# Other due times for visits, block sums and first halves, and other normalisers for five groups, in a planned attention and feed-forward kernel

## The chip, the cores and the metric

The kernel runs on one core of a Trainium2 chip. The time is device microseconds of that core for one execution. Before the change it was 583.85 us, the median of three runs (583.55 to 584.67).

## The reference

Attention over 4 batches of 8 heads, 768 tokens and 64 numbers a head, then a feed-forward part over the 3072 tokens with 512 features and 2048 hidden ones. All inputs are float32.

```python
k_sum = k.reshape(B, H, nb, block, D).max(axis=3)      # block = 32
v_sum = v.reshape(B, H, nb, block, D).mean(axis=3)
scores_l = scale * np.matmul(q, k.transpose(0, 1, 3, 2))
mask_l = np.abs(pos[:, None] - pos[None, :]) < window   # window = 16
scores_s = scale * np.einsum('bhsd,bhnd->bhsn', q, k_sum) + np.log(block)
scores_all = np.concatenate([np.where(mask_l, scores_l, -1e9), scores_s], axis=-1)
a = np.exp(scores_all - np.max(scores_all, axis=-1, keepdims=True))
a = a / (np.sum(a, axis=-1, keepdims=True) + 1e-09)
x = np.matmul(a, np.concatenate([v, v_sum], axis=2))    # then tokens x 512
h = x @ w_in
r = np.maximum(h, 0.0)
out = (r * r) @ w_out
```

## The kernel before, in words

The 3072 tokens are cut into 48 groups of 64. Eight groups make a unit of 512 tokens. A *visit* on TensorE does the scores of coming groups (L756) and the values of earlier ones (L997) in one go. Around a visit the other engines work on a group: the vector engine masks the scores and takes the row maximum (L830), ScalarE takes exponentials (L887), the vector engine the reciprocal of the sum (L899, L900). Then a group is normalised, either by one vector instruction (L906) or by four on ScalarE (L913); the string `NORMAL_BY` has a letter for each of the 48 groups, D or A. The result is turned for the next matmul, by TensorE and a copy (L926, L933) or by the vector engine and DMAs (L955, L970, L975). The outcome of a visit is cut into a high part `xh` (ScalarE, L1062) and a low part `xl` (vector engine, L1065).

The feed-forward matmuls are of high and low parts in three terms, to keep float32's precision. The first two units, called plain, go through 16 tiles f of the hidden features. For each there are 12 hidden matmuls (L1195) into one of two PSUM banks `h`; ScalarE applies relu (`rl`, L1204), squares in place (L1205) and makes the high part `gh` (L1206); the vector engine makes the low part `gl` from both (L1209); 12 outer matmuls (L1219) follow. There is one buffer `rl`: relu of the next tile can start only when `gl` of this one is done. The visits' results and the groups turned on TensorE use the two PSUM banks of `h` too. The remaining four units go by a scheme with fewer matmuls that needs sums of blocks of the weights (L1731 and L1514). These sums are made while the plain units run: GpSimd adds whole blocks (L1300, L1315), ScalarE and the vector engine split them (L1318, L1321); half sums (L1364, L1379) are GpSimd's for five of the eight pairs and the vector engine's for pairs 4, 6 and 7 (`HALF_SUMS_BY`), split at L1382 and L1385; SP stores them (L1324, L1390) in device memory. In the same stretch the weights come in (L1125) and are split (L1128, L1131, L1137, L1142, L1145), and the keys' block maxima are taken (L566).

In what order an engine does all this is not written by hand. Every piece of work is given to a planner (class `Plan`) with an engine, an estimated duration, the work it comes after, the buffers it takes and a *due time*. The planner plays the program through: whenever an engine is free, it starts the ready piece with the earliest due time. The result is one fixed order for each engine, which the chip keeps: a piece that isn't ready holds up all behind it on its engine. The due times come from tables of numbers in us: `VISITS` (visits, and with them all work on their groups), `COMBS` (block sums of pairs, L1288), `SUMS` (half sums, L1916), `HALF_AT` (the first halves of the first unit, L1105 and L1176), `FV_AT` (loads of the values of the later batches, L597), `Q_LEAD` (query loads, L1747) and `X_LEAD` (splits of a visit's outcome, L1085). A changed number moves whatever takes part in the same competition, also work that the table doesn't name.

```python
t2 = add(f"RL{name}", "ACT", act, lambda: nc.scalar.activation(cut(r), cut(h), AF.Relu), due + 3, [t1], take=[r], use=[h])
...
if NORMAL_BY[g] == "A":
    t_n = add(f"N{g}", "ACT", 1.2, normal_by_act, due - 10, [t_r], use=[pr, nm])
else:
    t_n = add(f"N{g}", "DVE", 0.56, normal, due - 10, [t_r], use=[pr, nm])
```

Of the kernel before, what the change touches and what calls it, by code (L numbers as in the profile page):

```python
# [44 lines left out]
HIGH_DVE = 0  # L45
ONE_EXP = 1
RUN1, RUN2, RUN4 = (1 + 218 / n for n in (1024, 2048, 4096))
NORMAL_BY = "DDDDDDDDDDDDAADDDDDAADDADDAAAADDADDDDAADAAAAAAAA"
HALF_SUMS_BY = "PPPPDPDD"
TURN_BY = "PPPPDPDDPDDDDDDDDDDDDDDD"  # L50
LAG = 2
PLAIN = 2
RINGED = 4
PRODUCTS = 7
FV_AT = 60.61, 233.96
FV1_LEAD = 17.0
HALVED = 2
TURN_LATE = 0.4
COMBS = 113.9, 126.8, 141.39, 159.1, 177.9, 210.24, 223.15, 214.82
Q_LEAD = 10.72  # L60
XS_LEAD = 10
R_LEAD = 9
TR_LEAD = 16.82
VISITS = 50.65, 58.31, 70.31, 76.15, 99.76, 110.62, 136.36, 142.89, 161.01, 177.12, 203.05, 215.03, 227.83, 233.26, 248.89, 277.47, 296.02, 310.51, 324.02, 346.69, 366.69, 366.74, 394.74
X_LEAD = 5.36
SPLIT_AT = -7.62
KEPT = 105.02, 3.08
GH_LEAD = 12
# [258 lines left out]
def attention_then_relu2_ffn(  # L327
# [96 lines left out]
    T0, SLOW, STEP = 28.0, 6.4, 6.7  # L424
    MIXED_STEP = 1.54, 1.41
    X_BY = 19.41, 14.78
    SUMS = 121.7, 129.74, 148.43, 166.33, 195.88, 201.13, 197.53, 197.25, 153.98, 169.96, 168.64, 165.29, 173.06, 198.45, 180.64, 190.85
    PRODUCT_STEP = 1.51, 1.34
    A0, A1, B0, B1 = 12.0, 2.0, 21.0, 2.2
    HALF_AT = 26.97, 32.0  # L430
    MX = 0.95
    steps = [SLOW, STEP]
    unit_at, mixed_at, products_at, at = [], [], [], T0
# [11 lines left out]
    def wanted(g):  # L445
# [5 lines left out]
        if g < APART:  # L451
            return VISITS[i] if g % 2 else (VISITS[i] + (VISITS[i - 1] if i else VISITS[0] - 20)) / 2
        return VISITS[i - 1] + 17 - 5 * (g % 2 == 0)

# [3 lines left out]
    def visited(g):  # L458

        return VISITS[(g - UG) // 2 + (g >= APART - 2)] if g >= UG else wanted(g)  # L460

# [134 lines left out]
    def batch_v(b):  # L596
        key = FV_AT[b - 2] if b > 1 else visited(b * NW - 1) - FV1_LEAD if b else -60  # L597
        out_ps = h_buf(f"vps{b}")
# [207 lines left out]
    def softmax(g, by_pe=False):  # L806
# [107 lines left out]

        if NORMAL_BY[g] == "A":
            t_n = add(f"N{g}", "ACT", 1.2, normal_by_act, due - 10, [t_r], use=[pr, nm])
# [86 lines left out]
    def visit(both, then=(), block_sums=None):  # L1003

        n, g = len(both), (both or (-1,))[-1]
        due = visited(g) if both else VISITS[(then[0] - UG) // 2 - 1]
        x_ps = h_buf(f"x{g}") if n == 2 else x_buf(f"x{g}") if n else None
# [278 lines left out]
    def combine(p):  # L1286

        due = COMBS[p]  # L1288
        ws = [woven[1, 2 * p + k] for k in range(2)]
# [374 lines left out]
    def mixed(s):  # L1664
# [26 lines left out]
        def product(p, j, o, begins, deps, also=(), taken=False):  # L1691
# [54 lines left out]
            n += 1  # L1746
            return t, due + 1.5 - Q_LEAD  # L1747

# [165 lines left out]
    for p in FOLDED:  # L1914
        for k in range(2):
            combine_in(p, k, SUMS[2 * p + k])  # L1916
    for s in range(NS):
# [69 lines left out]
```

## Time and profile before

| | us |
|---|---|
| median of three runs | 583.85 |
| the profiled execution | 583.48 |
| its span, first to last instruction | 581.0 |
| TensorE busy | 563.0 (97%) |
| vector engine busy | 452.2 (78%) |
| ScalarE busy | 373.7 (64%) |
| GpSimd busy | 134.5 (23%) |
| mean granted clock of TensorE | 0.996 |

The span is the profile's; 2.48 us of the execution's own time lie around it. A row of a timeline gives the start in us, the time until the last instruction of the row ended, the engine, the line, the operation, output and inputs with their shapes, and how many instructions the row holds. What stands in brackets is the idle time of the engine ahead of the row and what ended it. PE is TensorE, DVE the vector engine, ACT ScalarE, POOL GpSimd, SPq the queue of SyncE, which issues the DMAs. The plain units run from about 30 to 260 us, the rest behind.

### The profile page before, as it was taken

The page shows a single profiled execution, that of the slowest core. Times are in us where ns is not written, and L with a number is a line of the kernel's source. Part 1 is how long each engine was busy: PE and PEld are TensorE (multiplying, and loading weights), DVE is VectorE, ACT ScalarE, POOL GpSimd, SP SyncE. Part 2 cuts the span into 40 slices and gives each one's busy share as a digit, 9 for nine tenths or more (in the row PEclk, how much of TensorE's full clock was granted, in tenths as well). Part 3 has the DMA queues.
Part 4 walks back from the last instruction along what each step waited for, and adds up shares of the span by engine and source line. Part 5 has one row for each costly group of instructions (what it writes and reads, how often), then busy time and mean ns, then how long its engine had stood idle before and what let it go on. Part 6 is the DMA issues. An engine that isn't in the chain of part 4 may idle for free.

```text
span 581.0 us, 12047 instructions
## 1 busy us (share of the span) xinstructions
PE 563.0 (97%) x4052; PEld 460.2 (79%) x4052; DVE 452.2 (78%) x1015; ACT 373.7 (64%) x968; POOL 134.5 (23%) x193
## 2 busy tenths in 40 slices
PE   7879999999999899999999999999999999999997
PEld 6668787888887688887888888888888888888885
DVE  4899999685799997879976978869932656868864
ACT  1899899786757787768765768464634642454442
POOL 4300010167669469500043430000000000000000
PEclk9999999999999999999999999999999999999999
DMA  8899996989997999999988888866875566667672
GB/s 298 295 382 340 332 337 243 323 327 341 304 381 236 327 358 338 364 333 335 312 271 246 268 257 257 268 181 192 256 240 175 178 195 192 196 195 226 196 227 98
DMA packets 88082, 157.15 MB, mean 270 GB/s; under 512 B 9066, under 2 KB 30926, under 8 KB 88022
## 3 DMA queue, kind: packets, MB, share of 16 engines
q1 hardware_dynamic: 88022, 156.39, 82.2%
q8 instruction: 32, 0.52, 0.4%
q14 instruction: 28, 0.23, 0.1%
HBM read 111.30 MB, written 44.66 MB: 268 GB/s over the span
## 4 chain that ended last, share of the span: by engine, by line
PE 76%; DVE 9%; DMA 8%; SPq 3%; issue 2%; ACT 1%; DVEq 0%; ACTq 0%
PE o L1514 23%; PE o L1731 14%; PE h L1195 9%; PE o L1219 9%; PE sz L1731 8%; PE att L1514 4%; PE x L997 3%; DMA raw<-wW 3%; PE att L756 2%; PE sa L1731 2%; PE att L1731 2%; DMA v<-vS 1%; DMA fv_lent<-vS 1%; DMA out<-os 1%; DVE ci L1379 1%
## 5 line engine op out<-in xcount | busy, mean ns | idle before, releaser
L1496 ACT CAST gh<-g 128x512 fp32r<-128x512 f32 x112 | 69.3, 621 | 63.2 <-DVE gl L1501 30.5
L1514 PE MATMUL o<-gh,w 128*128 128x512 f32 x384 | 103.0, 390 | 0.0
L1501 DVE TENSOR_TENSOR gl<-g,gh 128x512 fp32r<-128x512 f32 x112 | 76.8, 693 | 22.9 <-ACT gh L1496 22.4
L1514 PEld LDWEIGHTS o<-gh,w 128*128 128x128 f32 x384 | 71.8, 188 | 15.0
L1195 PE MATMUL h<-xh,w 128*128 128x512 f32 x240 | 76.2, 399 | 3.9 <-ACT rl L1204 3.9
L1768 ACT ACTIVATE g<-g 128x512 f32<-128x512 f32 x60 | 37.6, 630 | 49.5 <-DVE g L1764 49.3
L887 ACT ACTIVATE p<-p,small 128x118 f32<-128x118 f32 x160 | 61.1, 387 | 1.6 <-DVE small L830 1.6
L1219 PE MATMUL o<-w,gh 128*128 128x512 f32 x240 | 61.9, 394 | 0.0
L1514 PE MATMUL o<-gl,w 128*128 128x512 f32 x192 | 59.2, 389 | 0.0
L1195 PEld LDWEIGHTS h<-xh,w 128*128 128x128 f32 x240 | 45.1, 191 | 14.2 <-ACT rl L1204 4.7
L1219 PEld LDWEIGHTS o<-w,gh 128*128 128x128 f32 x240 | 44.4, 188 | 9.7 <-issue 0.4
L1195 PE MATMUL h<-xl,w 128*128 128x512 f32 x120 | 47.2, 394 | 0.0
L1514 PEld LDWEIGHTS o<-gl,w 128*128 128x128 f32 x192 | 36.0, 188 | 7.6
L1731 PE MATMUL o<-w,w 128*128 128x512 f32 x160 | 40.6, 390 | 0.0
L769 POOL COPY kb<-kb 128x96 f32<-128x96 f32 x25 | 10.9, 435 | 107.1 <-PE att L756 36.4
L1774 POOL TENSOR_TENSOR g<-g 128x512 f32<-128x512 f32 x16 | 22.6, 1418 | 53.7 <-ACT g L1768 53.1
L1731 PEld LDWEIGHTS o<-w,w 128*128 128x128 f32 x160 | 30.0, 188 | 6.3
L1491 DVE TENSOR_TENSOR g<-g 128x512 f32<-128x512 f32 x48 | 33.9, 716 | 1.2 <-POOL g L1774 0.7
L830 DVE CUSTOM_DVE_ANT_0 p<-att,mask 128x118 f32<-128x118 f32 x152 | 32.5, 272 | 2.6 <-PE att L756 2.6
L1731 PE MATMUL sz<-xh,w 128*128 128x512 f32 x128 | 34.5, 391 | 0.0
L1219 PE MATMUL o<-w,gl 128*128 128x512 f32 x120 | 33.6, 389 | 0.0
L1764 DVE CUSTOM_DVE_ANT_0 g<-sz,g 128x512 f32<-128x512 f32 x32 | 21.9, 685 | 13.2 <-ACT g L1751 6.4
(201 smaller groups left out, 1186.7 us busy)
## 6 DMA issues: line engine op xcount, KB each, us to landing
raw<-wW SPq DMA_DIRECT2D x32, 512.0 KB
w<-scr_t SPq DMA_DIRECT2D x64, 256.0 KB
w<-scr_s SPq DMA_DIRECT2D x64, 256.0 KB
w<-scr_a SPq DMA_DIRECT2D x48, 256.0 KB
w<-scr_i SPq DMA_DIRECT2D x44, 256.0 KB
turn<-a SPq DMA_DIRECT2D x18, 512.0 KB
scr_t<-ci SPq DMA_DIRECT2D x16, 512.0 KB
v<-vS SPq DMA_DIRECT2D x34, 192.0 KB
```

The source lines that it names most:

```text
L830: nc.vector.tensor_tensor_reduce(out=pr.tile[:, j, :KEYS], in0=score_at(g, 0, j), in1=mask_of(g)[0], scale=-SCALE, scalar=-NEG, op0=ALU.ad ...
L887: nc.scalar.activation(x, score_tile(g, p % parts)[:, p] if by_pe else x, AF.Exp, bias=nm.tile[:, p : p + 1], scale=SCALE if by_pe else -1 ...
L1195: nc.tensor.matmul(cut(h), lhsT=lhs.tile[:, k // 2, k % 2 * P : (k % 2 + 1) * P], rhs=rhs[:, k, c0 : c0 + n], start=(i == 0), stop=(i == 3 ...
L1219: nc.tensor.matmul(o_of(o, t).rearrange("p (h c) -> p h c", h=2), lhsT=terms[i][0].tile[:, (t - t0) * P : (t - t0 + 1) * P], rhs=terms[i][ ...
L1491: lambda x=x, ins=ins, op=op: nc.vector.tensor_tensor(out=x.tile, in0=ins[0].tile, in1=ins[1].tile, op=op),
L1496: f"GH{s}_{n}", "ACT", 0.54, lambda x=x, gh=gh: nc.scalar.copy(out=gh.tile, in_=x.tile), due - GH_LEAD, ready,
L1501: lambda x=x, gh=gh, gl=gl: nc.vector.tensor_tensor(out=gl.tile, in0=x.tile, in1=gh.tile.bitcast(F32), op=ALU.subtract),
L1514: nc.tensor.matmul(o.tile[:, d], lhsT=chunk.tile[:, w * HALF + d * P : w * HALF + (d + 1) * P], rhs=y.tile, start=begins and w == 0 and y ...
L1731: nc.tensor.matmul(o.tile, lhsT=lhs(w, k), rhs=y[k], start=begins and i == 0, stop=i == 5, skip_group_check=not begins,)
L1764: lambda: nc.vector._custom_dve(TENSOR_ADD_SAT, out=to.tile, in0=o.tile, in1=x.tile, s0=HUGE, s1=0.0), key, deps,
L1768: f"G{name}_{s}", "ACT", 0.63, lambda: nc.scalar.activation(to.tile, to.tile, AF.Square), key + 0.7, [t], use=[to]
L1774: f"{name}_{s}", engine, cost, lambda: tensor.tensor_tensor(out=to.tile, in0=a.tile, in1=b.tile, op=ALU.subtract), key, deps,
```

## The change

Only numbers of the tables and five letters change; the instructions on TensorE are as many as before. Groups 12, 27, 28, 46 and 47 are normalised by the vector engine instead of ScalarE. `FV_AT` goes from 60.61, 233.96 to 53.99, 235.63; `Q_LEAD` from 10.72 to 9.51; `X_LEAD` from 5.36 to 6.51; the tenth of `SUMS` from 169.96 to 176.4; `HALF_AT` from 26.97 to 23.74 in its first number. Five of the eight `COMBS` become 3.87 to 8.79 earlier. Of `VISITS`, five get later by 0.94 and two earlier by 5.33 and 0.2.

```diff
-NORMAL_BY = "DDDDDDDDDDDDAADDDDDAADDADDAAAADDADDDDAADAAAAAAAA"
+NORMAL_BY = "DDDDDDDDDDDDDADDDDDAADDADDADDADDADDDDAADAAAAAADD"
...
-FV_AT = 60.61, 233.96
+FV_AT = 53.99, 235.63
...
-COMBS = 113.9, 126.8, 141.39, 159.1, 177.9, 210.24, 223.15, 214.82
-Q_LEAD = 10.72
+COMBS = 113.9, 126.8, 132.6, 155.23, 174.03, 206.37, 219.28, 214.82
+Q_LEAD = 9.51
```

What this does to the order is seen in three places. The names in the rows are the program's tiles: `gl_4` is the low part of hidden tile f = 4, the last number only counts the tiles of the whole program and differs between the two kernels; `kb` holds the keys and their block maxima, `raw`, `t` and `w` are weights on the way, `ci` the half sums, `cr` and `cs` the block sums.

The first place is the vector engine in the first unit. Before, at `gl_4`:

```order
L906 TENSOR_TENSOR p_82<-p_82,small_87 128x4x118
L1137 SCALAR_TENSOR_TENSOR t_929<-t_929,raw_811 128x1024
L899 TENSOR_SCALAR small_88<-small_88 128x4
L900 RECIPROCAL small_88<-small_88 128x4
L566 TENSOR_REDUCE kb<-kb 128x24
L906 TENSOR_TENSOR p_83<-p_83,small_88 128x4x118
L566 TENSOR_REDUCE kb<-kb 128x24 x2
L1209 TENSOR_TENSOR gl_4_1078<-rl_4_1045,gh_4_1060 128x512
L566 TENSOR_REDUCE kb<-kb 128x24
```

Now:

```order
L1137 SCALAR_TENSOR_TENSOR t_939<-t_939,raw_812 128x1024
L906 TENSOR_TENSOR p_83<-p_83,small_88 128x4x118
L1145 TENSOR_TENSOR w_1019<-t_915,w_1019 128x4x256
L1131 TENSOR_SCALAR raw_876<-raw_876 128x1024
L566 TENSOR_REDUCE kb<-kb 128x24
L1209 TENSOR_TENSOR gl_4_1083<-rl_4_1033,gh_4_1067 128x512
L566 TENSOR_REDUCE kb<-kb 128x24 x2
L1145 TENSOR_TENSOR w_1058<-t_939,w_1058 128x4x256
L566 TENSOR_REDUCE kb<-kb 128x24
```

The second and third key reductions have moved behind `gl_4`, and a weight piece ahead of the first.

The second place is the vector engine in the second unit, at `gl_3`, ahead of the first masking (L830) of the groups of one visit. Before:

```order
L1209 TENSOR_TENSOR gl_2_2245<-rl_2_2207,gh_2_2238 128x512
L566 TENSOR_REDUCE kb<-kb 128x24 x3
L1209 TENSOR_TENSOR gl_3_2280<-rl_3_2248,gh_3_2277 128x512
L1364 TENSOR_TENSOR ci_0_2286<-w_1133 128x2x128
L1364 TENSOR_TENSOR ci_0_2286<-w_1179 128x2x128
L1379 TENSOR_TENSOR ci_0_2286<-ci_0_2286 128x128 x4
L1385 TENSOR_TENSOR ci_0_2286<-ci_0_2286 128x4x128
L1209 TENSOR_TENSOR gl_4_2353<-rl_4_2288,gh_4_2351 128x512
L1321 TENSOR_TENSOR cr_2274<-cr_2274 128x2x256
L830 ISA p_82,small_72<-att_68,mask_76 128x118
```

Now:

```order
L1209 TENSOR_TENSOR gl_2_2251<-rl_2_2212,gh_2_2239 128x512
L1364 TENSOR_TENSOR ci_0_2255<-w_1149 128x2x128
L1364 TENSOR_TENSOR ci_0_2255<-w_1216 128x2x128
L1379 TENSOR_TENSOR ci_0_2255<-ci_0_2255 128x128 x4
L566 TENSOR_REDUCE kb<-kb 128x24
L1209 TENSOR_TENSOR gl_3_2285<-rl_3_2257,gh_3_2280 128x512
L1385 TENSOR_TENSOR ci_0_2255<-ci_0_2255 128x4x128
L1209 TENSOR_TENSOR gl_4_2348<-rl_4_2306,gh_4_2313 128x512
L830 ISA p_82,small_72<-att_68,mask_76 128x118
```

The half sums of pair 4 stand ahead of `gl_3` instead of behind it, two of the three reductions have gone to an earlier place, and the block-sum remainder `cr` (L1321) has gone behind the masking. The buffer of these half sums is the one that held the third and fourth output piece of the first unit (stored at L1262) before, and now the one that held the first and second.

The third place is some 35 us further on in the second unit, at `gl_7` on the vector engine. Before:

```order
L1379 TENSOR_TENSOR ci_0_2566<-ci_0_2566 128x128 x4
L955 STREAM_TRANSPOSE a_2609<-p_83 128x4x128
L1364 TENSOR_TENSOR ci_0_2657<-w_1684 128x2x128
L1364 TENSOR_TENSOR ci_0_2657<-w_1665 128x2x128
L1385 TENSOR_TENSOR ci_0_2566<-ci_0_2566 128x4x128
L1379 TENSOR_TENSOR ci_0_2657<-ci_0_2657 128x128 x4
L1209 TENSOR_TENSOR gl_7_2672<-rl_7_2614,gh_7_2659 128x512
L1321 TENSOR_TENSOR cr_2499<-cr_2499 128x2x256
```

Now:

```order
L1385 TENSOR_TENSOR ci_0_2419<-ci_0_2419 128x4x128
L1379 TENSOR_TENSOR ci_1_2569<-ci_1_2569 128x128 x4
L1321 TENSOR_TENSOR cr_2497<-cr_2497 128x2x256
L1321 TENSOR_TENSOR cs_2498<-cs_2498 128x2x256
L1385 TENSOR_TENSOR ci_1_2569<-ci_1_2569 128x4x128
L1364 TENSOR_TENSOR ci_0_2633<-w_1591 128x2x128
L1209 TENSOR_TENSOR gl_7_2699<-rl_7_2637,gh_7_2657 128x512
L1379 TENSOR_TENSOR ci_0_2633<-ci_0_2633 128x128 x4
```

The four sums of pair 7 (L1379, the last `ci`) have moved behind `gl_7`, the two remainders `cr` and `cs` of pair 4 ahead of it. On ScalarE, which does relu of tile 8 after `gl_7`, stood before:

```order
L913 ACTIVATE p_83<-p_83,small_72 128x118 x4
L1205 ACTIVATE rl_7_2614<-rl_7_2614 128x512
L1318 CAST cr_2499<-cr_2499 128x2x256
L1382 CAST ci_0_2566<-ci_0_2566 128x4x128
L1206 CAST gh_7_2659<-rl_7_2614 128x512
L1318 CAST cs_2500<-cs_2500 128x2x256
L1382 CAST ci_0_2657<-ci_0_2657 128x4x128
L1204 ACTIVATE rl_8_2709<-h_8_2616 128x512
```

and now:

```order
L1382 CAST ci_0_2419<-ci_0_2419 128x4x128
L1318 CAST cs_2498<-cs_2498 128x2x256
L1204 ACTIVATE rl_7_2637<-h_7_2543 128x512
L1205 ACTIVATE rl_7_2637<-rl_7_2637 128x512
L1206 CAST gh_7_2657<-rl_7_2637 128x512
L1382 CAST ci_1_2569<-ci_1_2569 128x4x128
L1204 ACTIVATE rl_8_2705<-h_8_2608 128x512
```

The normaliser of group 27 (L913) has gone from ScalarE, and the cast of pair 7's half sums has moved behind `rl_8`.

## Rows read from the trace of the kernel before

**Rows 1.** Part 1 of the page: busy time, share of the span, and instructions.

```profile
PE 563.0 (97%) x4052; PEld 460.2 (79%) x4052; DVE 452.2 (78%) x1015; ACT 373.7 (64%) x968; POOL 134.5 (23%) x193
```

**Rows 2.** The table of windows, of stretches chosen by hand. Columns: stretch, its length, busy time and instructions of PE, PEld, DVE, ACT and POOL, granted clock of TensorE, share of the DMA engines' time, GB/s.

```profile
45.00:75.00 30.00, 29.19 (x160) 23.69 (x159) 29.90 (x59) 27.93 (x62) 0.00 (x0) 1.00 0.95 342
...
135.00:165.00 30.00, 30.00 (x242) 24.56 (x241) 22.96 (x65) 22.91 (x68) 19.95 (x26) 1.00 0.93 317
...
195.00:210.00 15.00, 12.28 (x103) 9.84 (x102) 14.71 (x50) 13.81 (x44) 4.22 (x6) 0.89 0.90 316
...
345.00:576.00 231.00, 231.00 (x1127) 191.05 (x1120) 162.08 (x258) 112.08 (x203) 2.97 (x3) 1.00 0.69 207
```

**Rows 3.** What TensorE waited for: line, releaser, us in total, times, longest.

```profile
PE h L1195 <- ACT rl L1204: 3.9, 3, 2.7
...
PE o L1731 <- DVE g L1764: 0.3, 1, 0.3
```

**Rows 4.** The timeline of TensorE, 185 to 206 us.

```profile
185.29 0.73 PE L1195 MATMUL h<-xh,w 128*128 128x512 f32 x2 [0.37 <-ACT rl L1204]
...
190.86 0.62 PE L1195 MATMUL h<-xh,w 128*128 128x512 f32 x2
...
193.58 0.62 PE L1219 MATMUL o<-w,gh 128*128 128x512 f32 x2
...
201.23 1.22 PE L1195 MATMUL h<-xh,w 128*128 128x512 f32 x2 [2.72 <-ACT rl L1204]
...
205.62 0.63 PE L1219 MATMUL o<-w,gh 128*128 128x512 f32 x2
```

**Rows 5.** The timeline of ScalarE, 199 to 201 us.

```profile
199.92 0.62 ACT L1382 CAST ci<-ci 128x512 fp32r<-128x512 f32 x1 [1.00 <-DVE ci L1379]
200.58 0.60 ACT L1204 ACTIVATE rl<-h 128x512 f32<-128x512 f32 x1
```

**Rows 6.** The timeline of the vector engine, 173 to 202 us.

```profile
173.41 0.95 DVE L1321 TENSOR_TENSOR cr<-cr 128x512 fp32r<-128x512 f32 x1
174.28 0.27 DVE L830 CUSTOM_DVE_ANT_0 p<-att,mask 128x118 f32<-128x118 f32 x1
...
180.79 1.67 DVE L906 TENSOR_TENSOR p<-p,small 128x472 f32<-128x472 f32 x1
...
185.75 0.69 DVE L1065 TENSOR_TENSOR xl<-x,xh 128x512 fp32r<-128x512 f32 x1 [0.33 <-ACT xh L1062]
...
190.56 1.96 DVE L1379 TENSOR_TENSOR ci<-ci 128x128 f32<-128x128 f32 x4
...
197.64 0.71 DVE L1364 TENSOR_TENSOR ci<-w 128x256 f32<-128x256 f32 x2
...
198.88 1.01 DVE L1379 TENSOR_TENSOR ci<-ci 128x128 f32<-128x128 f32 x4
199.81 0.68 DVE L1209 TENSOR_TENSOR gl<-rl,gh 128x512 fp32r<-128x512 f32 x1
200.41 0.68 DVE L1321 TENSOR_TENSOR cr<-cr 128x512 fp32r<-128x512 f32 x1
```

**Rows 7.** The timelines of TensorE and of the vector engine, 30 to 42 us.

```profile
30.34 0.63 PE L926 MATMUL t<-ident,qvpa_lent 128*128 128x128 f32 x4 [1.76 <-DVE qvpa_lent L906]
...
40.89 0.64 DVE L906 TENSOR_TENSOR p<-p,small 128x472 f32<-128x472 f32 x1
41.44 0.41 DVE L1065 TENSOR_TENSOR xl<-att,xh 128x256 fp32r<-128x256 f32 x1
...
41.03 0.50 PE L1195 MATMUL h_0b<-xh,w 128*128 128x256 f32 x2 [1.65 <-ACT xh L1062]
```

**Rows 8.** Groups of instructions: line, engine, operation, tiles, count | busy us, mean ns of one | idle before.

```profile
L913 ACT ACTIVATE p<-p,small 128x118 f32<-128x118 f32 x80 | 24.8, 384 | 3.3 <-DVE small L900 3.3
...
L906 DVE TENSOR_TENSOR p<-p,small 128x472 f32<-128x472 f32 x20 | 17.4, 870 | 0.1
```

**Rows 9.** The timeline of all engines, 66 to 70 us.

```profile
66.71 1.80 DVE L566 TENSOR_REDUCE kb<-kb 128x24 f32<-128x768 f32 x2
...
68.43 0.68 DVE L1209 TENSOR_TENSOR gl<-rl,gh 128x512 fp32r<-128x512 f32 x1
...
69.14 0.60 ACT L1204 ACTIVATE rl<-h 128x512 f32<-128x512 f32 x1 [1.88 <-DVE gl L1209]
...
69.79 0.50 PE L1195 MATMUL h<-xh,w 128*128 128x512 f32 x1 [0.81 <-ACT rl L1204]
```

**Rows 10.** The timeline of the vector engine where it takes up the weight pieces of f = 12.

```profile
84.80 0.69 DVE L1131 TENSOR_SCALAR raw<-raw 128x1024 uint32<-128x1024 uint32 x1
```

**Rows 11.** The timelines of SP's queue, GpSimd and the vector engine, 159 to 195 us, at the half sums.

```profile
159.09 1.94 SPq L1262 DMA_DIRECT2D out<-os  x4
...
164.12 1.30 POOL L1300 TENSOR_TENSOR cr<-w 128x512 f32<-128x512 f32 x1 [7.24 <-PE o L1219]
...
166.50 1.78 DVE L1364 TENSOR_TENSOR ci<-w 128x256 f32<-128x256 f32 x2 [0.53 <-DMA out<-os]
168.31 2.92 DVE L1379 TENSOR_TENSOR ci<-ci 128x128 f32<-128x128 f32 x4
...
192.25 2.50 POOL L1379 TENSOR_TENSOR ci<-ci 128x128 f32<-128x128 f32 x4
```

**Rows 12.** The timeline of TensorE at the visit behind the half sums.

```profile
169.41 0.63 PE L756 MATMUL att<-kb,q 64*64 64x118 f32 x16
```

More of the change, by code (lines that the diff above doesn't have):

```diff
@@ L63 @@
 TR_LEAD = 16.82
-VISITS = 50.65, 58.31, 70.31, 76.15, 99.76, 110.62, 136.36, 142.89, 161.01, 177.12, 203.05, 215.03, 227.83, 233.26, 248.89, 277.47, 296.02, 310.51, 324.02, 346.69, 366.69, 366.74, 394.74
-X_LEAD = 5.36
+VISITS = 50.65, 58.31, 70.31, 76.15, 99.76, 111.56, 137.3, 143.83, 161.95, 178.06, 203.05, 215.03, 227.83, 233.26, 248.89, 277.47, 296.02, 305.18, 323.82, 346.69, 366.69, 366.74, 394.74
+X_LEAD = 6.51
 SPLIT_AT = -7.62
@@ L426, in attention_then_relu2_ffn @@
     X_BY = 19.41, 14.78
-    SUMS = 121.7, 129.74, 148.43, 166.33, 195.88, 201.13, 197.53, 197.25, 153.98, 169.96, 168.64, 165.29, 173.06, 198.45, 180.64, 190.85
+    SUMS = 121.7, 129.74, 148.43, 166.33, 195.88, 201.13, 197.53, 197.25, 153.98, 176.4, 168.64, 165.29, 173.06, 198.45, 180.64, 190.85
     PRODUCT_STEP = 1.51, 1.34
     A0, A1, B0, B1 = 12.0, 2.0, 21.0, 2.2
-    HALF_AT = 26.97, 32.0
+    HALF_AT = 23.74, 32.0
     MX = 0.95
```

## Prediction

> **What bounds the kernel now.** I read the busy shares first, then the windows, the waits of TensorE, and last the timelines at each wait. TensorE is busy 563.0 us of a span of 581.0 [rows 1], so the whole room of a change that leaves the matmuls alone is the 18 us in which it idles, plus what it loses at a lower clock. The windows say where [rows 2]: from 345 to 576 it is busy all the time; from 195 to 210 it works 12.28 of 15 us at a granted clock of 0.89, the only window below 1.00. The waits say for whom [rows 3]: one hidden matmul waited 2.7 us for ScalarE's `rl`. The timeline has it at 201.23 [rows 4]. The `rl` that it waited for ran at 200.58, behind ScalarE's `ci` cast at 199.92, which had itself waited 1.00 us for the vector engine's `ci` sums [rows 5]. Beside this ScalarE wait stands a harder one: `rl` has one buffer, which only the vector engine's `gl` frees, and that `gl` ran from 199.81 to 200.49 [rows 6]. So both causes end within 0.6 us of each other, and taking ScalarE's away alone would bring 0.1 us. Behind the `gl` lies a vector engine that was busy from 174.28 to 200.49, with 0.33 us of idle time in 26.21 [rows 6]. What has to come earlier is this row of work.
>
> The clock's price: the hidden visit after the wait took 205.62 - 201.23 = 4.39 us, against 193.58 - 190.86 = 2.72 for one at full clock, with the same 12 matmuls [rows 4]. That is 1.67 us, so the place costs 2.72 + 1.67 = 4.39 us. The waits of 1.76 and 1.65 us at the start were followed by no fall: the window from 45 on stands at 1.00 [rows 2, 7].
>
> **The change, part by part.** Instructions on TensorE are as many as before. Five groups have their normalising moved from ScalarE (four instructions of 384 ns, 1.5 us) to the vector engine (one of 870 ns) [rows 8]: 4.4 us more on the one, 7.7 less on the other. Both have room on average; only 27 stands where an engine is waited for.
>
> 1. Start (30 to 45). The second `xl` ends at 41.85, and the first-half matmuls wait for both [rows 7]. In the new order the normaliser between the two (0.64) goes behind, but two small instructions for a reciprocal come in, some 0.4: about -0.25 us. Bounds: 0 (the cast that feeds it is also late, behind an `rl`) and -1.65 (the whole wait).
>
> 2. The wait of 0.81 us at 69.79. ScalarE's `rl` waited 1.88 for `gl_4`, which stood behind two key reductions of 1.80 us in all [rows 9]. The new order sets `gl_4` ahead of these two. It can then end near 67.3, `rl` near 68.0, and TensorE comes free at 68.98 (69.79 - 0.81): the wait goes, -0.81, and nothing else is late there. Bounds 0 and -0.81. After this TensorE is 1.06 us early. I cost the rest to 155 at nothing: the window from 135 to 165 has it busy for all of its 30 us, with the vector engine busy for 22.96 [rows 2], and that spare time covers the moved work; the 1.5 MB of values that SP now issues ahead of two weight pieces are 4.4 us at the 342 GB/s of [rows 2]; of the two weight pieces the vector engine took up the first at 84.80, without an idle moment ahead of it [rows 10], so they had landed by then and have time to spare.
>
> 3. The half sums of the fifth pair (lines 1364 and 1379) and `gl_3`, 160 to 175. Before, `gl_3` ran ahead of them; now they and a reduction run ahead of it. They took 1.78 us at 166.50 and, from 168.31 to 171.23, 2.92 [rows 11]; the same at 197.64 and 198.88 took 0.71 and 1.01 [rows 6]. GpSimd was at work in the first case and had ended at 194.75 in the second [rows 11]. So the price ahead of `gl_3` lies between 1.72 and 4.70 us, and the reduction adds 0.90 (half of 1.80, [rows 9]). GpSimd begins its next sums at 164.12 when a matmul ends [rows 11], now near 163.0. The half sums' buffer was one that the third and fourth output store set free, and is now that of the first two. SP issued the four from 159.09, and the sums at 166.50 had waited for the last [rows 11]. The first two had landed by 164.12, since GpSimd's sum there wrote where they had read. In the new order they are issued about 1.5 us earlier (1.06 by the shift, 0.4 because one key load less stands ahead), so they land by 162.6. I take 161.5: the pair runs before GpSimd is at work, the four partly beside it, and `gl_3` ends near 166. Its `rl` follows 0.7 later, and TensorE needs it when the visit at 169.41 [rows 12], now 168.35, begins: no wait. Bounds: none, and the 5.4 us of the slower rival.
>
> A page of the Trainium skill speaks against this step: GPSIMD Engine Reference, section 8 "Key points", says that GpSimd shares its SBUF interfaces with VectorE, so that vector instructions with two SBUF inputs contend with it. The two durations of the four `ci` instructions, 2.92 beside GpSimd and 1.01 without it, agree. If all of the sums here were to run beside GpSimd, the page would have `gl_3` end near 168.3 and the visit wait 0.6 us, and the sum below would be 0.6 us less.
>
> 4. The row of work from the visit to `gl_7`. With the half sums out of the way the first masking begins when the visit's scores are there, about 0.95 us into it: 169.3 instead of 174.28. Between the masking and the end of `gl_7` the vector engine loses the four `ci` sums of 1.01, and gains a block-sum remainder that stood ahead of it (0.95 at 173.41), the normaliser of group 27 (0.87) and two more remainders (0.60 each, as from 199.81 to 200.41) [rows 6, 8]: 26.21 - 1.01 + 0.95 + 0.87 + 1.20 = 28.2 us, to 197.5. Bounds: 26 (the normaliser at 180.79 and the four sums at 190.56, 1.67 and 1.96, at the 0.64 of 40.89 and the 1.01 of 198.88, and 27's at 0.64 too) and 29 (27's at 1.67) [rows 6, 7], that is 195.3 to 198.3. Some waits for ScalarE and GpSimd will come in between, so I take 198.0, near the upper end. ScalarE's `rl_8` now stands directly behind a cast and no longer behind the last `ci` cast or the normaliser, so it ends at 198.7 and the matmuls start at 198.75.
>
> 5. The wait of 0.37 us at 185.29 [rows 4], for an `rl` whose `gl` belongs to the same row of work, goes: -0.37. TensorE comes to the place of [rows 4] at 198.51 - 1.06 - 0.37 = 197.1 (its wait before began at 201.23 - 2.72 = 198.51) and waits 1.65 us in place of 2.72. Earlier by 201.23 - 198.75 = 2.48 in all.
>
> 6. The clock. A wait of 1.65 lies next to the 1.76 and 1.65 that kept the clock [rows 7], and far from 2.72: I take it that it stays, -1.67. Bounds 0 and -1.67.
>
> 7. Behind it. The 0.3 us wait of a mixed product [rows 3] comes later in a row that is now ahead: -0.3, bounds 0 and -0.3. From 345 on there was no idle time to win, and 162.08 of 231 us of the vector engine were busy [rows 2], so the two normalisers there find room; if one of them delays a `gl`, that is up to 0.87.
>
> Sum: -2.48 - 1.67 - 0.3 = -4.45, from the profiled execution's own 583.48 us (span 581.0 and 2.48 around it) to 579.0. That execution lies 0.37 below the median of the runs shown, 583.85, so the median should come to 579.4. The likeliest case's own range is 578 to 580.5.
>
> **The rivals.**
> - *The clock falls all the same, or the wait comes out near 2.5.* The row of [rows 4] shows a fall after 2.72 and none after 1.76; what lies between is not shown. -2.48 - 0.3: 581.1 at the median.
> - *All the waits in the two plain units go.* If the vector engine's row from 169.3 needs 27 us or less, `rl_8` is there at about 197. -(0.25 + 0.81 + 0.37 + 2.72 + 1.67 + 0.3) = -6.12: 577.7. For it: [rows 11] show GpSimd's sums slowing the vector engine, and these now begin and end earlier. Against it: three pieces of work more stand ahead of `gl_7`.
> - *The half sums come late and hold everything: slower.* If the first output stores land only near 166.4, as the last did, the sums run wholly beside GpSimd: 166.50 + 1.78 + 2.92 + 0.90 and a `gl` of 0.68 to 0.95 put the end of `gl_3` near 173, its `rl` at 173.7, and the visit of 168.35 waits 5.4 us. The wait is longer than the 2.72 that brought the clock down, so 1.67 or more come on top, and the vector engine's row starts at 175, as late as before, with 2 us more in it. TensorE gets to the later place at 197.1 + 5.4 = 202.5, and the matmuls start near 203.6: +2.4, with the second fall of the clock up to +4. 586.3 to 587.9, say 587. It decides from a landing of about 163.4: from there `gl_3` is late by 2 to 3 us, and that with the clock's fall eats the 4.4. For it: the sums now wait for a transfer, with a DMA share of 0.93 from 135 to 165 [rows 2], and everything on the vector engine is in order. Against it: TensorE is earlier there, and the two stores are the first of four.
> - *The change does nothing that counts.* Rows are set anew in some hundred places, and new waits of a few tenths appear where the order was tight; the one at 201.23 stays at 2.7: 583.5 to 584.
>
> **How the numbers follow.** Forecast 0.43, clock falls 0.20, all gone 0.13, nothing 0.08, slower 0.16. A measurement of this kernel can tell about 0.2% from no change, 1.2 us: the limits are 582.7 and 585.0. The first three cases are faster, 0.76; the fourth is the same, 0.08; the last slower, 0.16. The range leaves out about the slower case and the lowest edge of the third: 577.3 to 584.2. The predicted time is that of the likeliest case, 579.4.
>
> **What would show it.** Right: no wait of TensorE near 69; `gl_3` of the second unit ending before 168 and no wait of the visit near 168; first masking of that visit near 169; the hidden visit after the next but one starting near 198.8 with a wait under 2 us, and a granted clock of 1.00 in the window around 200. Wrong: a granted clock below 0.95 around 200; a wait for `out<-os` on the vector engine past 163; a wait of TensorE for `gl` or `gh` behind 345, where there was none; or new waits of more than 1 us between 75 and 160, which I cost at nothing.

## The result, and the profile after

The change made the kernel slower: 588.27 us at the median of 16 runs (586.37 to 592.43), against 584.64 for the kernel before (583.55 to 588.96, 16 runs). The ratio is 1.0055, with a 95% interval of 1.0031 to 1.0080. Runs of one and the same kernel scatter over some 5 us here, so ratios with intervals carry the reading below, and a profiled execution is used for where time goes, not for how much. The profiled execution of the changed kernel, 592.34 us, is one of its longest; the one of before, 583.48, one of the shortest. Of one experiment, e_sums, the profiled execution was a disturbed one (594 us), and no time of it is read.

The page's first part and the windows of the changed kernel, with the columns of [rows 1, 2]:

```profile
PE 568.9 (96%) x4052; PEld 465.1 (79%) x4052; DVE 455.7 (77%) x1020; ACT 369.6 (63%) x948; POOL 136.0 (23%) x193
```

```profile
105.00:135.00 30.00, 28.19 (x230) 22.58 (x229) 20.27 (x59) 21.51 (x60) 10.73 (x14) 0.94 0.94 327
...
195.00:210.00 15.00, 11.60 (x98) 8.92 (x97) 14.41 (x50) 9.62 (x30) 2.92 (x5) 0.89 1.03 345
...
240.00:345.00 105.00, 100.85 (x799) 82.20 (x799) 82.40 (x222) 70.44 (x216) 25.91 (x23) 0.97 0.89 281
345.00:576.00 231.00, 231.00 (x1128) 190.90 (x1127) 163.22 (x264) 112.53 (x202) 5.17 (x4) 1.00 0.73 215
```

The window around 200 is as before (clock 0.89, 11.60 us busy where 12.28 were). Two new ones have idle time and a lower clock: 105 to 135, and 240 to 345. (From 0 to 45 the clock was 0.96, where it was 1.00; the last section takes this up.) Behind 345 nothing is lost, as before. TensorE's waits, of at least 1 us and new or changed:

```profile
PE o L1731 <- ACT os L1256: 4.1, 1, 4.1
...
PE h L1195 <- ACT rl L1204: 2.4, 1, 2.4
...
PE t L926 <- DVE small L899: 1.5, 1, 1.5
...
PE o L1219 <- DVE gl L1209: 1.0, 1, 1.0
```

The timeline of TensorE has them at four places; [rows 4, 7, 12] answer to these rows:

```profile
30.33 0.63 PE L926 MATMUL t<-ident,qvpa_lent 128*128 128x128 f32 x4 [1.72 <-DVE qvpa_lent L906]
...
118.78 0.63 PE L926 MATMUL t<-ident,p 128*128 128x128 f32 x4 [1.46 <-DVE small L899]
...
172.27 0.63 PE L756 MATMUL att<-kb,q 64*64 64x118 f32 x16
...
199.08 1.20 PE L1219 MATMUL o<-w,gl 128*128 128x512 f32 x4 [0.99 <-DVE gl L1209]
...
204.74 0.73 PE L1195 MATMUL h<-xh,w 128*128 128x512 f32 x2 [2.41 <-ACT rl L1204]
...
265.31 1.22 PE L1731 MATMUL o<-xh,w 128*128 128x512 f32 x2 [4.15 <-ACT os L1256]
```

I followed how far TensorE was from the kernel before at points where both had the same matmuls behind them; "early" and "late" mean this in what follows. It was 1.04 us early at 109, 2.87 late at 130, 3.50 late at 209 and 9.46 late at 281; nothing changed from there to the end. So two groups turned at 118.78 cost 3.9 us (1.46, a following 0.35, and a clock of 0.66 from 120 to 125); the place at 200 was about as dear as before; and the first mixed product at 265.31 cost 4.15 and about 2 us of clock.

Why these two waits came is seen on the vector engine, its timeline at the three places:

```profile
108.14 0.70 DVE L1131 TENSOR_SCALAR raw<-raw 128x1024 uint32<-128x1024 uint32 x1 [3.26 <-DMA turn<-a]
...
111.67 1.23 DVE L1145 TENSOR_TENSOR w<-t,w 128x1024 fp32r<-128x1024 f32 x1 [1.11 <-ACT w L1142]
...
117.46 1.17 DVE L906 TENSOR_TENSOR p<-p,small 128x472 f32<-128x472 f32 x1
...
165.76 0.76 DVE L1364 TENSOR_TENSOR ci<-w 128x256 f32<-128x256 f32 x2 [0.72 <-DMA out<-os]
166.56 3.22 DVE L1379 TENSOR_TENSOR ci<-ci 128x128 f32<-128x128 f32 x4
...
170.56 1.13 DVE L1209 TENSOR_TENSOR gl<-rl,gh 128x512 fp32r<-128x512 f32 x1
...
173.67 1.00 DVE L1209 TENSOR_TENSOR gl<-rl,gh 128x512 fp32r<-128x512 f32 x1 [0.83 <-ACT gh L1206]
174.59 0.27 DVE L830 CUSTOM_DVE_ANT_0 p<-att,mask 128x118 f32<-128x118 f32 x1
...
203.29 0.68 DVE L1209 TENSOR_TENSOR gl<-rl,gh 128x512 fp32r<-128x512 f32 x1
...
262.72 0.69 DVE L1256 COPY os<-o 128x512 f32<-128x512 f32 x1 [3.51 <-DMA scr_s<-cr]
```

At 108 the weight pieces of f = 15 now stand ahead of the masking of two groups, and their transfer landed only at 108.1. The row names `turn<-a`; ScalarE's row of the same moment names the weights themselves:

```profile
108.09 1.20 ACT L1128 ACTIVATE t<-raw 128x1024 f32<-128x1024 f32 x1 [3.95 <-DMA raw<-wW]
```

At 262.72 the first output piece of the second unit is to be copied out of PSUM, and its buffer is one that the block sums of pair 6 held. The store of these sums, which has to have read it, was issued on SP's queue at 257.87:

```profile
251.02 2.00 SPq L975 DMA_DIRECT2D a<-turn  x4
253.21 0.35 SPq L697 DMA_DIRECT2D q<-qW  x1
254.60 0.33 SPq L708 DMA_DIRECT2D v<-vS  x1
256.00 0.35 SPq L697 DMA_DIRECT2D q<-qW  x1
257.45 0.32 SPq L708 DMA_DIRECT2D v<-vS  x1
257.87 0.39 SPq L1324 DMA_DIRECT2D scr_s<-cr  x1
```

It stands behind the turned reads, two query and two value loads. In the kernel before it stood ahead of them and was issued at 247.03, and the copy into the buffer waited for no store:

```profile
247.03 0.49 SPq L1324 DMA_DIRECT2D scr_s<-cr  x1
...
255.27 0.65 DVE L1256 COPY os<-o 128x512 f32<-128x512 f32 x1
```

The sums themselves were later too: GpSimd ended them at 247.3 in the changed kernel, after it had stood still for 14.53 us until a store of half sums had landed:

```profile
212.60 1.01 POOL L1364 TENSOR_TENSOR ci<-w 128x256 f32<-128x256 f32 x1 [14.53 <-DMA scr_t<-ci]
...
246.61 0.73 POOL L1315 TENSOR_TENSOR cs<-cs,cr 128x256 f32<-128x256 f32 x1
```

In the kernel before it ended them at 241.2:

```profile
240.02 1.19 POOL L1315 TENSOR_TENSOR cs<-cs,cr 128x256 f32<-128x256 f32 x1
```

### The profile page after: what moved, and what is told of

It reads as the page before. It is cut to its first block, busy times and chain, and to the rows that moved or that the text cites. A ratio compares the mean times of both kernels' runs of the same rounds, so it can differ in the third digit from the quotient of the medians.

```text
span 590.5 us, 12024 instructions
## 1 busy us (share of the span) xinstructions
PE 568.9 (96%) x4052; PEld 465.1 (79%) x4052; DVE 455.7 (77%) x1020; ACT 369.6 (63%) x948; POOL 136.0 (23%) x193
## 4 chain that ended last, share of the span: by engine, by line
PE 72%; DMA 10%; DVE 7%; ACT 4%; SPq 4%; issue 2%; POOL 1%; ACTq 0%; DVEq 0%; POOLq 0%
PE o L1514 22%; PE o L1731 14%; PE sz L1731 7%; PE h L1195 7%; PE o L1219 7%; PE att L1514 4%; PE x L997 2%; PE sa L1731 2%; PE att L756 2%; DMA raw<-wW 2%; PE att L1731 2%; DMA qvpa_lent<-vF 2%; DMA scr_s<-cr 2%; DMA a<-turn 1%; DMA out<-os 1%
## 5 line engine op out<-in xcount | busy, mean ns | idle before, releaser
L1219 PE MATMUL o<-w,gh 128*128 128x512 f32 x240 | 63.1, 400 | 0.0
L769 POOL COPY kb<-kb 128x96 f32<-128x96 f32 x25 | 12.7, 508 | 110.2 <-PE att L756 36.0
L1731 PE MATMUL o<-xh,w 128*128 128x512 f32 x112 | 31.8, 408 | 4.1 <-ACT os L1256 4.1
L830 DVE CUSTOM_DVE_ANT_0 p<-att,mask 128x118 f32<-128x118 f32 x152 | 32.5, 273 | 1.0 <-PE att L756 1.0
```

The lines of the kernel that those rows point to most:

```text
L769: nc.gpsimd.tensor_copy(out=kb[:, :, nxt : nxt + NB], in_=kb[:, :, k0 : k0 + NB])
L830: nc.vector.tensor_tensor_reduce(out=pr.tile[:, j, :KEYS], in0=score_at(g, 0, j), in1=mask_of(g)[0], scale=-SCALE, scalar=-NEG, op0=ALU.ad ...
L1219: nc.tensor.matmul(o_of(o, t).rearrange("p (h c) -> p h c", h=2), lhsT=terms[i][0].tile[:, (t - t0) * P : (t - t0 + 1) * P], rhs=terms[i][ ...
L1731: nc.tensor.matmul(o.tile, lhsT=lhs(w, k), rhs=y[k], start=begins and i == 0, stop=i == 5, skip_group_check=not begins,)
```

## The experiments

Most of them take the planned order of a kernel and set a few named pieces of work elsewhere in it, the rest as it was. The code for it stands where the order is played out:

```diff
-        for t in plan.order():
+        tasks = plan.order()
+        for names, place in (
+            (("WS6_0", "WS6_1"), "SL6_1"),
+        ):
+            moved = [next(t for t in tasks if t.name == name) for name in names]
+            tasks = [t for t in tasks if t not in moved]
+            at = [t.name for t in tasks].index(place) + 1
+            tasks[at:at] = moved
...
+        for t in tasks:
```

Names: WS6 are the two stores of the block sums of pair 6, SL6 their low parts; GL1_6, RL1_7, SQ1_7, GH1_7 are `gl`, relu, square and `gh` of tiles 6 and 7 of the second unit; WR, WM, WJ, WH, WW the steps in the splitting of a weight tile (L1131, L1128, L1137, L1142, L1145). Medians in us, and ratios to the kernel before, run beside it:

| kernel | median | ratio, 95% interval |
|---|---|---|
| changed (e_again) | 588.55 | 1.0067 (1.0040 to 1.0094) |
| e_weights | 587.90 | 1.0055 (1.0028 to 1.0082) |
| e_store | 584.89 | 1.0003 (0.9979 to 1.0026) |
| e_gl | 587.45 | 1.0048 (1.0022 to 1.0074) |
| e_all | 584.17 | 0.9989 (0.9964 to 1.0013) |
| e_all2 | 585.64 | 1.0007 (0.9988 to 1.0026) |
| e_sums | 585.35 | 1.0014 (0.9991 to 1.0037) |
| e_sums_w | 584.85 | 1.0000 (0.9975 to 1.0025) |
| e_half | 590.14 | 1.0104 (1.0080 to 1.0129) |
| e_before_gl | 585.29 | 1.0019 (0.9998 to 1.0040) |
| e_before_store | 587.76 | 1.0047 (1.0022 to 1.0073) |

**e_again: the changed kernel unaltered.**

> The changed kernel once more, unaltered. Its profiled execution (592.34 us) was among the longest of its 16 runs (586.37 to 592.43), so it may hold waits that a usual run doesn't. Theory A: three places cost time in every run, the turn of two groups at 118.78 (1.46 + 0.35 us and a clock fall), the two waits at 199.08 and 204.74 (0.99 + 2.41 and a clock fall) and the wait of 4.15 us at 265.31 with a clock fall; then a second profile shows all three and 590 us or more. Theory B: the places at 118 and 200 are fixed by the order, and the wait at 265 depends on when one store of block sums lands and is there in the longest runs alone; then a profile of a run near 587 to 588 shows the first two and no wait above 1 us near 265.

Its profiled execution took 586.68 us. TensorE's timeline:

```profile
117.46 0.63 PE L926 MATMUL t<-ident,p 128*128 128x128 f32 x4 [0.54 <-DVE small L899]
...
200.31 1.07 PE L1195 MATMUL h<-xh,w 128*128 128x512 f32 x2 [2.52 <-ACT rl L1204]
...
260.56 1.20 PE L1731 MATMUL o<-xh,w 128*128 128x512 f32 x4 [3.83 <-ACT os L1256]
```

Neither theory as it stood: the wait of about 4 us at 260 is there in a short run too, so it is not one of the longest runs alone; the one at 118 shrank to 0.54 without a fall of the clock (0.78 in e_store, 1.51 in e_gl), so that one is what varies. Up to the place at 260 this run had lost nothing: TensorE was 0.83 us early at 257, and 3.80 late at 281.

**e_store: the two stores of pair 6 earlier on SP's queue** (the diff above).

> The changed kernel with the two stores of the block sums of pair 6 (line 1324) issued on SP's queue ahead of the turned reads and the query and value loads of the next groups instead of behind them; nothing else moves. Theory: the copy of the first output piece at 262.72 waited for the buffer that these stores read, and they stood 7 us in SP's queue; then no wait near 265, and the longest runs (590 and above) go; the median comes down by 0.5 to 2 us if the wait is in some runs alone, by 5 to 6 if in all. Rival: the wait is for the sums themselves, which GpSimd ends at 247.3 in place of 241.2; then the wait stays above 2 us.

The stores were issued at 251.12 and the wait was gone, on SP's queue and on TensorE:

```profile
251.12 0.43 SPq L1324 DMA_DIRECT2D scr_s<-cr  x1
251.66 0.43 SPq L1324 DMA_DIRECT2D scr_s<-cs  x1
```

```profile
260.20 1.20 PE L1731 MATMUL o<-xh,w 128*128 128x512 f32 x4 [0.15 <-ACT os L1256]
```

GpSimd ended the sums at 246.3 in this run, 5 us later than in the kernel before, and still the copy did not wait for the stores. So the place in the queue made the wait, not the sums. The median fell by 3.7 us against the same kernel unaltered, to a ratio of 1.0003: as far as the interval tells, this one place holds the whole loss.

**e_before_store: the kernel before, with these two stores set behind the loads.**

```diff
+            (("WS6_0", "WS6_1"), "LV33"),
```

> The kernel before the change with one thing of the change: the two stores of the block sums of pair 6 issued behind the query, value and turned reads of the next groups on SP's queue, as the changed kernel has them; nothing else moves. Theory: this order alone makes the wait. The loads ahead were issued until 254.8 in the kernel before, so the stores land near 259 where the first output copy stood at 255.27: a wait of 3 to 4 us of TensorE near 257 and a clock fall of 1.5 to 2 behind it, the median 4 to 6 us above before. Rival: in the changed kernel the sums of pair 6 were also 6 us later on GpSimd, and that is the cause; then the wait here is under 2 us and the time within 2 us of before.

The output copy on the vector engine, and the product on TensorE behind it:

```profile
257.21 0.69 DVE L1256 COPY os<-o 128x512 f32<-128x512 f32 x1 [3.06 <-DMA scr_s<-cr]
```

```profile
259.80 2.08 PE L1731 MATMUL o<-xh,w 128*128 128x512 f32 x4 [3.43 <-ACT os L1256]
```

The wait of 3 to 4 us is there, and the clock was 0.50 from 260 to 265. GpSimd's sums of pair 6 ended at 240.5 in this run, no later than in the kernel before, so the rival falls here too. The median rose by 3.3 us, just under the 4 to 6 expected; the ratio of 1.0047 is that of the change itself, within the intervals. The order of two transfers on SP's queue, put into the old kernel, does what the change did.

**e_weights: the weight pieces of f = 15 behind the masking and normalising.**

```diff
+            (("WM15",), "E16_3"),
+            (("WR15",), "M17b"),
+            (("WJ15",), "N16"),
+            (("WR14", "WH15", "WW15"), "N17"),
+            (("WM14",), "RL0_12"),
```

The last two also let the pieces of f = 14 (WR14, WM14) follow a little later, since their transfer lands later still.

> The changed kernel with the weight pieces of f = 15 (lines 1128, 1131, 1137, 1142, 1145) set behind the masking and the normalising of the two groups near 112, as before the change; nothing else moves. Theory: the two turns at 118.78 and 119.75 waited because the masking stands on the vector engine behind these pieces, and they behind a weight transfer that landed at 108. Then no wait of TensorE near 118, no clock fall at 120 to 125, and the time comes down by 3 to 4 us against the changed kernel (584 to 585). Rival: the masking is late because the visit is later in the new order and both engines are full; then the turns wait 1 us or more still and the time stays within 1 us of 588.

No wait near 118 and no lower clock there, as the theory has it, but the median came down by only 0.65 us, inside the scatter, as the rival has it. TensorE's timeline says where the gain went:

```profile
200.34 0.73 PE L1195 MATMUL h<-xh,w 128*128 128x512 f32 x2 [2.41 <-ACT rl L1204]
...
259.25 1.27 PE L1731 MATMUL o<-xh,w 128*128 128x512 f32 x4 [4.11 <-ACT os L1256]
```

TensorE was 2.43 us early at 130, where e_again has 0.04, but the matmuls at 200 begin at 200.34, where e_again has 200.31. The vector engine's half sums took 3.64 us here:

```profile
162.34 3.64 DVE L1379 TENSOR_TENSOR ci<-ci 128x128 f32<-128x128 f32 x4
```

In e_again the same four took 1.02:

```profile
163.14 1.02 DVE L1379 TENSOR_TENSOR ci<-ci 128x128 f32<-128x128 f32 x4
```

GpSimd was at work from 161.94 in e_weights and began only at 164.08 in e_again. `gl_7` ended at the same time in both, 199.6, and by 197 TensorE's lead had shrunk to 0.58, where e_again has 0.72, for the most part in waits of 0.4 to 0.7 us for relu and `gl`.

The wait near 260 is no floor that later work sets, as some expectations below call it: it was 4.11 us here and 3.83 in e_again, and what e_weights was ahead of e_again at 257, 1.6 us, was still 1.3 at 281. It comes on top, early or late.

**e_gl: `gl` of tiles 6 and 7 early, in the changed kernel.**

```diff
+            (("GL1_6", "RL1_7", "SQ1_7"), "GH1_6"),
+            (("GH1_7", "GL1_7"), "SCi6_0"),
```

> The changed kernel with gl of tiles 6 and 7 of the second unit (and the relu, square and high part of tile 7 on ScalarE) set as early as their inputs allow, ahead of a turn and of the half sums' remainders; nothing else moves. Theory: the waits at 199.08 and 204.74 come from the row of small work on the vector engine that stands ahead of these two; then both waits go, the clock stays at 1.00 there, and the time comes down by 0.99 + 2.41 + 1.67 = 4 to 5 us (583.5 to 584.5). Rival: the row is late since it began late, from the masking on; then the waits shrink by less than 1 us in all, and the clock falls.

```profile
201.19 0.73 PE L1195 MATMUL h<-xh,w 128*128 128x512 f32 x2 [0.70 <-ACT rl L1204]
...
215.17 0.73 PE L1195 MATMUL h<-xh,w 128*128 128x512 f32 x2 [0.76 <-ACT rl L1204]
...
261.02 2.08 PE L1731 MATMUL o<-xh,w 128*128 128x512 f32 x4 [4.22 <-ACT os L1256]
```

The wait at 199 went, that at 200 fell to 0.70 and the clock stayed at 1.00 there, and a new one of 0.76 came at 215: from 197 to 225 TensorE won 2.8 us on the kernel before. The wait of 4.22 with a clock of 0.50 behind it then cost 6.0 from 257 to 281, where e_again lost 4.6. The median is 1.1 us below e_again, inside the scatter; the expected 4 to 5 us did not come.

**e_all: the three edits together.**

> The changed kernel with all three of the earlier edits at once: the weight pieces of f = 15 behind the normalising, gl of tiles 6 and 7 early, the two stores of pair 6 ahead of the loads. Theory: the wait near 260 is a floor that later stores set, and it ate what the other two edits had won before it (each alone brought 0.5 to 1 us in place of 3 to 5). With the floor gone they show: 3.5 us for the store and 3 to 6 us more, 579 to 582. Rival: the gains before 260 are lost in other waits anyway; then the time is that of the store's edit alone, 584 to 585.5.

584.17 us, 0.9989 of the kernel before beside it (0.9964 to 1.0013). That is no longer slower, and not shown to be faster. The rival is nearer to it than the theory: beside e_store the other two edits brought 0.7 us of median, which the intervals do not tell from nothing. On TensorE:

```profile
200.40 1.07 PE L1195 MATMUL h<-xh,w 128*128 128x512 f32 x2 [1.83 <-ACT rl L1204]
...
257.12 1.20 PE L1731 MATMUL o<-xh,w 128*128 128x512 f32 x4 [0.32 <-ACT os L1256]
```

**e_all2: the same, with relu of tile 8 directly behind `gl` of tile 7.**

```diff
+            (("RL1_8", "SQ1_8"), "GL1_7"),
```

> The kernel with all three edits, and relu and square of tile 8 also directly behind gl of tile 7 on ScalarE (they stood behind a cast of half sums that waits for the vector engine). Theory: the wait of 1.83 us at 200.40 that was left there, with its clock fall, was this cast's, and goes: 1.8 to 3.5 us, 581 to 582.5. Rival: the work that is pushed back makes the next visit wait near 212 to 216, as in the kernel before with gl set early: 584 to 585.

```profile
209.79 3.60 PE L1219 MATMUL o<-w,gh 128*128 128x512 f32 x8 [2.04 <-ACT gh L1206]
```

The wait at 200 went, and one of 2.04 us with a clock of 0.66 behind it came at 209.79. The rival holds.

**e_before_gl: `gl` of tiles 6 and 7 early, in the kernel before.**

```diff
+            (("GL1_6",), "M27b"),
+            (("RL1_7", "SQ1_7", "GH1_7"), "N26"),
+            (("GL1_7",), "RCi6_0_1"),
+            (("RL1_8", "SQ1_8"), "N27"),
```

> The kernel before the change with gl of tiles 6 and 7 of the second unit, and the relu, square and high part that hang on them, as early as their inputs allow; nothing else moves. It tests what the prediction took for the bound of the kernel before. Theory: the wait of 2.72 at 201.23 goes with the clock's fall of 1.67 behind it, and as no later store waits here, the end comes earlier by 3 to 4.4 us: 580 to 581.5 where before has 584.6. Rival: the wait or the gain reappears elsewhere behind 205, as it did in the changed kernel; then 583.5 to 585.

```profile
212.60 1.15 PE L997 MATMUL x<-a,v 118*64 118x64 f32 x32 [1.62 <-ACT rl L1205]
...
216.17 1.22 PE L1195 MATMUL h<-xh,w 128*128 128x512 f32 x2 [2.41 <-ACT rl L1204]
```

The wait of 2.72 at 201.23 [rows 4] went, and 1.62 + 2.41 us came one visit later, with the clock at 0.67 from 215 to 225. TensorE was 3.93 us early at 212, much what the theory had to gain, and 2.79 late at 225. 585.29 us: nothing gained. What the prediction took for a wait that can be removed acted here as a debt of the vector engine and ScalarE from 165 to 215, which this order moved from one visit to the next.

**e_sums: one number, the tenth of SUMS, back at 169.96.**

```diff
-    SUMS = 121.7, 129.74, 148.43, 166.33, 195.88, 201.13, 197.53, 197.25, 153.98, 176.4, 168.64, 165.29, 173.06, 198.45, 180.64, 190.85
+    SUMS = 121.7, 129.74, 148.43, 166.33, 195.88, 201.13, 197.53, 197.25, 153.98, 169.96, 168.64, 165.29, 173.06, 198.45, 180.64, 190.85
```

> The changed kernel with one number taken back: the tenth of SUMS at 169.96 again (176.4 with the change), which is the due time of the second half sum of pair 4. In the planned order this sets that half sum back ahead of gl of tile 6, and the stores of pair 6 ahead of the query and value loads, as before the change. Theory: this number, by what it does to the order at these two places, is the main cause; no wait above 1 us near 260 and a median of 584 to 585.5. Rival: the stores are late for another reason (GpSimd's sums of pair 6 still end at 247 or later); then the wait of about 4 us stays and the time is 587 to 589.

585.35 us, the ratio 1.0014: the loss is gone but for what the interval leaves. The order on SP's queue has the two stores ahead of the query and value loads again. The next kernel has the same number taken back, and there they were issued from 245.86 and the output copy did not wait for them:

**e_sums_w: this number back, and the weight pieces behind the normalising.**

```diff
-    SUMS = 121.7, 129.74, 148.43, 166.33, 195.88, 201.13, 197.53, 197.25, 153.98, 176.4, 168.64, 165.29, 173.06, 198.45, 180.64, 190.85
+    SUMS = 121.7, 129.74, 148.43, 166.33, 195.88, 201.13, 197.53, 197.25, 153.98, 169.96, 168.64, 165.29, 173.06, 198.45, 180.64, 190.85
...
+            (("WM15",), "E16_3"),
...
+            (("WM14",), "RL0_12"),
```

> The changed kernel with the tenth of SUMS at 169.96 again and the weight pieces of f = 15 behind the normalising. What remains of the change is the start, the earlier gl_4, the half sums ahead of gl_3 and the normalisers. Theory: the predicted gain of about 1 us up to 110 and the earlier row of work at 160 now reach the end, since no later store waits: 582 to 584 (before 584.6 to 585.1). Rival: what is won before 200 is eaten by the vector engine's row from 165 to 215, which is as long as before: 584.5 to 585.5.

```profile
255.97 1.20 PE L1731 MATMUL o<-xh,w 128*128 128x512 f32 x4 [0.88 <-ACT os L1256]
...
263.62 1.36 PE L1731 MATMUL o<-xh,w 128*128 128x512 f32 x4 [1.91 <-DVE g L1764]
```

584.85 us, ratio 1.0000. What remains of the change is worth nothing that can be measured, and the time is the rival's. Its reason is not what the profile shows: TensorE was 3.21 us early at 212, so the row from 165 to 215 had not eaten the lead, and 1.23 late at 281. It was lost behind 225, in the two waits shown and a clock of 0.71 from 265 to 270.

**e_half: the first number of HALF_AT back at 26.97.**

```diff
-    HALF_AT = 23.74, 32.0
+    HALF_AT = 26.97, 32.0
```

> The changed kernel with the first number of HALF_AT taken back to 26.97. In the planned order the weight pieces of f = 15 go behind the masking and the normalising again, and the first halves as before; the stores of pair 6 stay behind the loads. Theory: no wait of TensorE near 118, but the wait near 260 stays, since it is a floor: 587 to 588.5, as with the weight pieces moved alone. Rival: the early order is what costs; then 585 or less.

590.14 us, above both expectations. The wait near 118 was gone and the one at the end of the unit stayed, as foreseen:

```profile
265.08 2.07 PE L1731 MATMUL o<-xh,w 128*128 128x512 f32 x4 [4.78 <-ACT os L1256]
```

But the old number under the other new ones makes a third order, with waits of 1 us and more at 169, 197 and 226 that neither kernel has. A part taken back tells of that part only where the order around stays the same; the edits of the order itself were the better instrument here.

## Why the prediction was wrong

The forecast was a gain of 4.45 us; the result is a loss of 3.6. The late store accounts for the loss. That the gain did not come either has a second reason, since e_store, without that wait, only stands level with the kernel before. Three of the signs that the prediction names for being wrong came: the clock of 0.89 around 200, a wait for `out<-os` that ended at 165.76, and the 1.46 us at 118.78. (Its base of 583.85 us, the median of three runs, also lay 0.8 below that of the 16.)

- **The part that failed is "Behind it", the seventh.** It looked at a wait of 0.3 us and at the room behind 345, and took it for granted that nothing between 210 and 345 got worse. The order of SP's queue near 250 had changed, and the store that an output buffer waits for had gone behind the turned reads, two query and two value loads. This is the 3 to 4 us of the result: 3.7 by e_store, 3.3 by e_before_store. The step was skipped, not mis-sized: the queue's order was compared only up to the first unit's weights and at the half sums.
- **"I cost the rest to 155 at nothing"** failed as well, in part of the runs: 1.46 + 0.35 us and a fall of the clock in one profile, 0.54 + 0.35 without one in the next. The cover named for it, spare time of the vector engine in a window, was no cover: the engine had idle time, 3.26 us just ahead of 108.14, but in order, behind a transfer, and the masking stood behind it.
- **The start and `gl_4`** came out in sum, 1.04 us early where 1.06 were summed, with no wait at 69.79, but in part by luck. At 45 TensorE was 0.42 early, in spite of a clock of 0.83 from 30 to 40 that nothing in the sum allows for, and 0.76 in e_again without that fall, where 0.25 were summed; from there to 109 it won some 0.6 in both where 0.81 were summed, since a wait of 0.26 (0.19 in e_again) came at 62.
- **The half sums ahead of `gl_3`** came out at the dear end in this profile and as forecast in e_again. The four took 3.22 us beside GpSimd (2.92 in [rows 11]), `gl_3` ended at 171.69, and its `rl` was done just as the visit at 172.27 began. No wait of TensorE, as forecast; the slower rival, which had its place here, is not what happened. In e_again the four were over as GpSimd began, and `gl_3` ended at 165.9, where "near 166" was forecast. On the page of the Trainium skill that was weighed (GPSIMD Engine Reference, section 8 "Key points"), which says that vector instructions with two SBUF inputs contend with GpSimd: the four had 3.22 us with GpSimd at work and 1.01 at 203.90 with GpSimd idle, which agrees.
- **The row from the masking to `gl_7`** was 203.97 - 174.59 = 29.4 us long, where 28.2 were summed, 28.7 taken (198.0 - 169.3) and 29 was the upper bound. It also began 2.32 us into the visit in place of 0.95, behind a `gl_4` that had waited 0.83 for ScalarE's `gh`. So the matmuls began 32.47 us behind the visit (204.74 - 172.27) in place of 30.40 (198.75 - 168.35), 2.07 later; TensorE itself came 1.31 later, 0.99 of it by the wait at 199.08. 1.65 + 2.07 - 1.31 is the 2.41 that was measured. In e_again the masking began with the scores, at 170.46; the row was 29.1 us long, and the wait 2.52.
- **The mechanism behind that term was wrong too.** The sum counted what a shorter wait there would bring to the end. In e_before_gl and e_all2 the wait removed at 200 came back at 209 to 216, in e_gl a part of it did, and in e_sums_w the lead won there was lost behind 225. So none of the orders tried brought the 4.39 us put down to this place to the end; that no order can is not shown.
- **The clock** fell at 204.74 (0.66 from 205 to 210), and the argument from the waits of 1.76 and 1.65 does not hold, as the last section shows.

What stays open: why single runs differ by 5 us (the opening alone, in the last section, makes up to 2.7 of it), and whether e_all is faster than the kernel before. Its interval reaches from 0.9964 to 1.0013.

## What to carry to other kernels

When an order is planned anew, go along each queue to its end for every piece that releases a buffer, transfers first: a store that slides behind loads costs nothing itself, and makes a copy wait whole microseconds later. A wait that an early step shortens is gained only if no later step is timed by another engine or queue; ask for each gain what times the next step. Where an engine is full over several visits, look whether setting one result earlier removes the wait or moves it on, as it did in e_before_gl and e_all2.

## What the runs showed of the hardware

The length of a wait did not decide here whether TensorE's granted clock fell. At the same place, the turns near 119, a wait of 1.46 us went with 0.66 from 120 to 125 in the changed kernel, and one of 1.51 in e_gl with 1.00. At 200, 2.41 us in e_weights left the clock at 1.00, and 1.83 in e_all brought 0.66. At 30, 1.76 in the kernel before [rows 7] and 1.72 in the changed one were followed by 1.00 and by 0.83 from 30 to 40. Every figure is one profiled execution.

The opening differs from run to run with the same instructions in the same order: the turn at 30 waited 1.72 us in one profile of the changed kernel and 1.08 in the next, and 2.63 in e_store, which changes nothing ahead of 250. At 45 TensorE stood 0.42 us early against the kernel before in the first, 0.76 early in the second and 0.79 late in the third; in e_weights, with the same opening, it was 1.88 early.

The same four vector instructions in the same order took 3.64 us in e_weights, beside GpSimd, and 1.02 in e_again, where GpSimd began as they ended: the price of a piece of work hung on when another engine began.
